# All K loads before all V loads in a decode-attention kernel, with one shared buffer pool and a split last V

## The chip, the cores and the metric

The kernel runs on one core of a Trainium2 chip. The metric is the device time of one execution in microseconds. Most executions of a kernel agree closely; a profiled execution also has a *span*, from its first to its last instruction, which in this case is 1.7 to 2.9 us shorter than the time of the same run. Times inside a run are counted from the start of its span; landings of loads are worked out from the semaphore marks in the trace, which the profile's own views do not list.

Short names: TensorE (PE) does matrix products, a *pair* is one weight load with its matmul; VectorE (DVE) and ScalarE (ACT) copy results and do the softmax; SyncE (SP) issues the loads; 16 DMA engines carry them out.

## The reference, cut to what matters

```python
B, D, Hq, Hkv, Sk, Dh = 32, 512, 32, 8, 2048, 128      # everything bfloat16
W = 512                                                # only the last 512 positions count
q = (x @ wq)                                           # 32 batches, one query each, 32 heads
k = k_cache[:, :, Sk - W:, :]; v = v_cache[:, :, Sk - W:, :]
p = softmax(q @ k.T * Dh ** -0.5)                      # 4 query heads share one K/V group
out = (p @ v) @ wo
```

Per batch 1 MB of K and 1 MB of V are read, besides 4 MB for wq and 4 MB for wo: 75.5 MB in all, each byte used once. Inside a group the 128 KB are contiguous; the kernel gives each of the 128 partitions four positions of a group, so a contiguous piece (a *row* of the load) is 1 KB.

## The kernel before

For every batch TensorE transposes K (32 pairs), VectorE and ScalarE copy the result (tile `kT_ps`) to `kT` (4 copies), and TensorE multiplies it with the queries (8 matmuls, "scores"). After every fourth batch (a *block*) the softmax runs on 128 rows at once, P is transposed (4 pairs), and PV is computed (32 pairs per batch). K and V have separate buffers, and their loads alternate:

```python
NK, NV = 4, 10                       # K buffers, V buffers, 1 MB each
# SyncE: k1, k2, k3, v0, k4, v1, ... then the last 5 K, then the last 8 V
for b in range(1, KSPLIT):           # KSPLIT = B - 5
    order.append(("k", b))
    if b >= VLAG: order.append(("v", b - VLAG))        # VLAG = 3
    if b == WO_AFTER: order.append(("wo", 0))          # WO_AFTER = 10
for b in range(KSPLIT, B): order.append(("k", b))
for b in range(KSPLIT - VLAG, B): order.append(("v", b))
# ... load_k(b) waits until K b-4 is transposed, load_v(b) until PV b-10 is done

# TensorE, program order
for s in range(0, 26):
    transposes(s + 2); scores(s)
    # s == 4*kb+4: ptrans(kb);  s == 4*kb+5: pv(kb), 4 batches at once
transposes(28); scores(26); oproj_A()                  # projection of batches 0 to 23
transposes(29); scores(27)
transposes(30); scores(28); ptrans(6)
transposes(31); scores(29); scores(30); scores(31)
pv(6); oprojT(6); ptrans(7); pv(7); oprojT(7)          # oprojT: 128 pairs for one block
out_transposes()
```

## Time and profile before

| | before |
|---|---|
| time, first four runs | 237.24 us median (237.09 to 238.6) |
| span of the profiled run | 234.7 us |
| TensorE matmul busy | 75% of the span |
| read from memory | 75.53 MB |

From the page: three rows of its slices (the span in 40 equal slices of 5.87 us: TensorE's granted clock in tenths, the busy share of the DMA engines in tenths, and GB/s), and the summary of the chain of work that ended last.

```profile
PEclk9975899989997558999799799979889999999755
DMA  6999999999999999999999999999999999999100
GB/s 214 413 393 348 350 349 348 351 348 348 351 353 348 349 348 351 349 349 349 349 350 348 351 348 350 348 350 348 349 350 348 350 349 349 348 338 339 64 6 1
...
DMA 56%; PE 36%; issue 3%; DVE 3%; SPq 0%; ACT 0%; DVEq 0%
```

The DMA engines have no pause from slice 2 to slice 37. With 8 KB rows (wq, slices 2 and 3) they move about 400 GB/s (418 to 430 between 8 and 14 us), with 1 KB rows 348 to 353 (338 and 339 in slices 36 and 37). Then come three slices with almost no load: a tail.

In the trace every load leaves 16 marks on its semaphore, and the kernel lets TensorE start on the data only when it has counted all 16. The marks of the last V load lie between 216.96 and 220.88 us (the prediction below has both 0.10 us later): the last mark is 3.9 us behind the first, and TensorE may start on this V only at 220.88. This spread, which the prediction calls skew, differs from load to load: 1.0 us for the load that landed at 25.7 us, 5.1 at most (landed at 206.2). The span ends at 234.7, 13.8 us later.

From the timeline of the kernel before, its end (columns: start us, duration us, engine, line, operation, output<-inputs, shapes, count; in brackets how long the engine idled before, and what released it):

```profile
210.71 5.13 PE L239 MATMUL sc_ps<-kT,L 128*128 128x512 bf16 x23
...
215.67 3.35 PE L268 MATMUL m_ps<-pT,vbuf 128*128 128x4 bf16 x128
...
219.41 3.56 PE L296 MATMUL m_ps<-oT_sb,wbuf 128*128 128x4 bf16 x128 [0.39 <-DVE oT_sb L450]
...
222.83 0.59 PE L253 MATMUL pT_ps<-ident,P 128*128 128x128 bf16 x4
223.45 0.60 ACT L381 ACTIVATE pT<-pT_ps 128x512 bf16<-128x512 bf16 x1 [5.89 <-PE pT_ps L253]
...
224.10 3.58 PE L268 MATMUL m_ps<-pT,vbuf 128*128 128x4 bf16 x128 [0.69 <-ACT pT L381]
...
228.07 3.58 PE L296 MATMUL m_ps<-oT_sb,wbuf 128*128 128x4 bf16 x128 [0.39 <-DVE oT_sb L450]
...
231.93 0.59 PE L309 MATMUL pT_ps<-ident,oT_sb 128*8 128x128 bf16 x4 [0.28 <-DVE oT_sb L458]
232.55 0.41 DVE L460 COPY out_sb<-pT_ps 8x512 bf16<-8x512 bf16 x1 [0.68 <-PE pT_ps L309]
232.99 0.31 SPq L169 DMA_DIRECT2D out_dram<-out_sb  x1
```

L239 is the score work of batches 29 to 31, L268 is PV of blocks 6 and 7, L296 the projection of a block, L253 the transposes of P. The scores end at 215.84. PV of block 7 starts at 224.10, three microseconds after its last V has landed. So the last byte is not what the end waited for: TensorE had its own queue of work, and it was late.

### The profile page before, as it was taken

How to read it: one execution, taken by the hardware profiler on the slowest of the kernel's cores; microseconds unless marked ns; L12 is line 12 of the kernel's file. 1: busy time of each engine (PE TensorE's matmuls, PEld its weight loads, DVE VectorE, ACT ScalarE, POOL GpSimd, SP SyncE). 2: the span in 40 equal slices, each digit the busy share in tenths (PEclk: the TensorE clock that was granted, in tenths of full speed). 3: DMA queues.
4: the chain of work that ended last, by engine and by line, in shares of the span. 5: the costliest groups of instructions: out<-in, count | busy, mean ns of one | idle time of the engine just before them, and what ended most of it. 6: DMA issues, size and time to landing. Idle time of an engine off the chain costs nothing.

```text
span 234.7 us, 6022 instructions
## 1 busy us (share of the span) xinstructions
PE 174.9 (75%) x2738; PEld 135.2 (58%) x2760; DVE 78.3 (33%) x147; ACT 46.3 (20%) x59; POOL 8.2 (4%) x9
## 2 busy tenths in 40 slices
PE   0606789689766019966996889669897699999985
PEld 0506767468544018744874567456865495675975
DVE  0303245532452003453334433453245330481101
ACT  2110331321132001132112221132033210141010
POOL 7600000000000000000000000000000000000000
PEclk9975899989997558999799799979889999999755
DMA  6999999999999999999999999999999999999100
GB/s 214 413 393 348 350 349 348 351 348 348 351 353 348 349 348 351 349 349 349 349 350 348 351 348 350 348 350 348 349 350 348 350 349 349 348 338 339 64 6 1
DMA packets 71308, 75.94 MB, mean 324 GB/s; under 512 B 1092, under 2 KB 70756, under 8 KB 70772
## 3 DMA queue, kind: packets, MB, share of 16 engines
q1 hardware_dynamic: 71252, 75.53, 99.9%
q8 instruction: 21, 0.34, 0.6%
q0 software_dynamic: 32, 0.03, 0.0%
q14 instruction: 3, 0.02, 0.0%
HBM read 75.53 MB, written 0.03 MB: 322 GB/s over the span
## 4 chain that ended last, share of the span: by engine, by line
DMA 56%; PE 36%; issue 3%; DVE 3%; SPq 0%; ACT 0%; DVEq 0%
DMA kbuf<-in_k_cache_dram 56%; PE sc_ps L239 10%; PE kT_ps L221 10%; PE m_ps L268 8%; PE m_ps L296 3%; PE sc_ps L282 3%; DVE kT L410 2%; PE sc_ps L198 1%; DVE oT_sb L450 0%; ACT pT L381 0%; PE pT_ps L309 0%; DVE out_sb L454 0%; SPq L141 0%; PE pT_ps L253 0%; SPq L122 0%
## 5 line engine op out<-in xcount | busy, mean ns | idle before, releaser
L221 PE MATMUL kT_ps<-ident,kbuf 128*128 128x128 bf16 x1024 | 73.7, 238 | 44.7 <-DMA kbuf<-in_k_cache_dram 41.9
L221 PEld LDWEIGHTS kT_ps<-ident,kbuf 128*128 128x128 bf16 x1024 | 67.8, 108 | 52.9 <-DMA kbuf<-in_k_cache_dram 48.4
L410 DVE COPY kT<-kT_ps 128x1024 bf16<-128x1024 bf16 x96 | 61.5, 686 | 81.5 <-issue 42.1
L239 PE MATMUL sc_ps<-kT,L 128*128 128x512 bf16 x234 | 59.4, 394 | 3.6 <-DVE kT L410 1.6
L355 ACT ACTIVATE kT<-kT_ps 128x1024 bf16<-128x1024 bf16 x32 | 32.7, 1023 | 137.5 <-PE kT_ps L221 119.5
L239 PEld LDWEIGHTS sc_ps<-kT,L 128*128 128x128 bf16 x256 | 25.2, 103 | 27.7 <-issue 5.8
L268 PEld LDWEIGHTS m_ps<-pT,vbuf 128*128 128x128 bf16 x1024 | 27.0, 97 | 2.6 <-ACT pT L381 1.0
L268 PE MATMUL m_ps<-pT,vbuf 128*128 128x4 bf16 x1024 | 27.0, 164 | 0.7 <-ACT pT L381 0.7
L450 DVE CAST oT_sb<-m_ps 128x128 bf16<-128x128 f32 x8 | 2.3, 292 | 36.4 <-PE m_ps L268 36.4
L432 DVE TENSOR_REDUCE mx<-sc_ps 128x1 f32<-128x512 f32 x8 | 5.5, 692 | 12.4 <-PE sc_ps L239 12.4
L367 ACT ACTIVATE E_sb<-sc_ps,nmx 128x512 f32<-128x512 f32 x8 | 5.5, 687 | 16.0 <-DVE nmx L434 16.0
L381 ACT ACTIVATE pT<-pT_ps 128x512 bf16<-128x512 bf16 x8 | 4.8, 597 | 15.3 <-PE pT_ps L253 15.3
L296 PE MATMUL m_ps<-oT_sb,wbuf 128*128 128x4 bf16 x256 | 7.1, 168 | 0.8 <-DVE oT_sb L450 0.8
L296 PEld LDWEIGHTS m_ps<-oT_sb,wbuf 128*128 128x128 bf16 x256 | 7.0, 103 | 0.9 <-DVE oT_sb L450 0.9
L282 PE MATMUL sc_ps<-wbuf,oT_sb 128*24 128x512 bf16 x32 | 7.1, 380 | 0.0
L190 PE MATMUL pT_ps<-ident,x_sb 32*128 32x32 bf16 x4 | 0.3, 182 | 7.6 <-DMA x_sb<-in_x_dram 7.6
L282 PEld LDWEIGHTS sc_ps<-wbuf,oT_sb 128*24 128x24 bf16 x32 | 3.7, 119 | 3.3 <-issue 0.4
L190 PEld LDWEIGHTS pT_ps<-ident,x_sb 32*128 32x128 bf16 x4 | 0.2, 102 | 7.6 <-issue 7.6
L443 DVE TENSOR_SCALAR P<-E_sb,rs 128x512 bf16<-128x512 f32 x8 | 3.9, 486 | 0.3
L424 DVE COPY L<-qT_sb 128x128 bf16<-128x128 bf16 x8 | 2.1, 262 | 4.5 <-ACT qT_sb L344 4.5
L439 DVE RECIPROCAL rs<-ssum 128x1 f32<-128x1 f32 x8 | 1.3, 164 | 6.8 <-ACT E_sb L367 6.8
L198 PEld LDWEIGHTS sc_ps<-xT_sb,wbuf 128*128 128x128 bf16 x128 | 3.5, 102 | 0.0
(22 smaller groups left out, 25.4 us busy)
## 6 DMA issues: line engine op xcount, KB each, us to landing
kbuf<-in_k_cache_dram SPq DMA_DIRECT2D x32, 1024.0 KB, 12.0
vbuf<-in_v_cache_dram SPq DMA_DIRECT2D x32, 1024.0 KB, 12.1
wbuf<-in_wq_dram SPq DMA_DIRECT2D x1, 4096.0 KB, 15.4
wbuf<-in_wo_dram SPq DMA_DIRECT2D x1, 4096.0 KB, 20.7
x_sb<-in_x_dram POOLq DMA_DIRECT2D x1, 32.0 KB, 6.2
out_dram<-out_sb SPq DMA_DIRECT2D x1, 24.0 KB
out_dram<-out_sb SPq DMA_DIRECT2D x1, 8.0 KB
```

The lines of the kernel that those rows point to most:

```text
L198: ins = pe.matmul(sc_ps[:, h * B:(h + 1) * B], wbuf[:, t * (H * DH) + h * DH: t * (H * DH) + (h + 1) * DH], xT_sb[:, t * B:(t + 1) * B], s ...
L221: ins = pe.transpose(dst, src, ident[:, :])
L239: ins = pe.matmul(sc_ps[:, half * 512:(half + 1) * 512], L[blk % 2][:, (bl * 8 + g) * 128:(bl * 8 + g + 1) * 128], kT_sb[b % NKT][:, g * W ...
L268: ins = pe.matmul(m_ps[:, reg * 128 + bl * 32 + 4 * g: reg * 128 + bl * 32 + 4 * g + 4], vbuf[vslot][:, g * W + j * 128: g * W + (j + 1) * ...
L282: ins = pe.matmul(sc_ps[0:NB_A, 512:1024], bass.AP(oT_sb, h, [[B * H, 128], [H, NB_A]]), wbuf[:, h * D:(h + 1) * D], start=(h == 0), stop= ...
L296: ins = pe.matmul(m_ps[:, c * 4 * NQ + 4 * q: c * 4 * NQ + 4 * q + 4], wbuf[:, h * D + c * 128: h * D + (c + 1) * 128], bass.AP(oT_sb, 4 * ...
L355: act.activation(kT_sb[b % NKT][:, c * 1024:(c + 1) * 1024], kT_ps[:, bank * 1024:(bank + 1) * 1024], ACTF.Copy,).then_inc(sem_act_kT, 1)
L367: act.activation(E_sb[:, :], sc_ps[:, half * 512:(half + 1) * 512], ACTF.Exp, bias=nmx[kb % 2][:, 0:1], scale=1.0, accum_out=ssum[kb % 2][ ...
L381: act.activation(pT_sb[kb % 2][:, :], pT_ps[:, 0:W], ACTF.Copy).then_inc(sem_act_pT, 1)
L410: dve.tensor_copy(kT_sb[b % NKT][:, c * 1024:(c + 1) * 1024], kT_ps[:, bank * 1024:(bank + 1) * 1024],).then_inc(sem_dve_kT, 1)
L432: dve.tensor_reduce(mx[kb % 2][:, 0:1], sc_ps[:, half * 512:(half + 1) * 512], AXX, ALU.max).then_inc(sem_dve_loc, 1)
L443: dve.tensor_scalar(P_sb[kb % 2][:, :], E_sb[:, :], rs[kb % 2][:, 0:1], None, ALU.mult).then_inc(sem_dve_P, 1)
```

## The change

Its intent: take all score and softmax work out of the end, so that after the last byte there is as little left as possible.

- All 32 K are loaded first, then wo, then all 32 V, from one pool of 14 buffers that K and V share.
- TensorE does all scores first. The transposed P of all 8 blocks is kept (8 buffers in place of 2), then PV follows for all batches. The last 8 batches get one output projection of 128 pairs in place of two, one for each block.
- The last four V are loaded by halves of the groups: first halves of all four, then second halves. This projection is done for the first 16 heads while the second halves arrive, and for the last 16 heads after that; VectorE adds the two parts.
- Max, exponential and normalisation of a block are placed one batch later.

```diff
-NK = 4
-NV = 10
+NKV = 14
...
-            # k and v alternate, the last 5 K before the last 8 V
+            for b in range(1, B):
+                load_k(b)
+            # wo here
+            for b in range(B - 4):
+                load_v(b)
+            for hf in range(2):
+                for q in range(4):
+                    b = B - 4 + q
+                    # groups 4*hf to 4*hf+3 of V b, own semaphore for each half
...
+            def wait_slot_free(i):              # i: 0..31 the K, 32..63 the V
+                j = i - NKV
+                if j < 0: return
+                if j < B: sp.wait_ge(sem_pe_kT, 4 * j + 4)        # K j transposed
+                else:     sp.wait_ge(sem_pe_pv, (j - B) + 1)      # PV j-32 done
...
             for s in range(0, B):
                 if s + LAGT < B: transposes(s + LAGT)      # LAGT = 2
                 scores(s)
-                # s == 4*kb+4: ptrans(kb);  s == 4*kb+5: pv(kb)
+                # s == 4*kb+5: ptrans(kb)
-            # late scores, oproj_A, pv(6), oprojT(6), ptrans(7), pv(7), oprojT(7)
+            ptrans(NBLK - 1)
+            for b in range(B - 4):
+                pv(b)
+                if b == 24: oprojT(0, 6)        # batches 0 to 23
+            for hf in range(2):
+                for b in range(B - 4, B):
+                    pv(b, range(4 * hf, 4 * hf + 4))
+                oproj_half(hf)                  # 16 heads, 8 batches: 64 pairs
             out_transposes()
...
-                    if b == 4 * kb + 5:         # VectorE: max of a block
+                    if b == 4 * kb + 3 + LAGT + 1:
```

More of the change, by code (lines that the diff above doesn't have):

```diff
@@ L15 @@
 NBLK = B // 4
-NK = 4
+NKV = 14
 NKT = 3
-NV = 10
 NKT_PS = 4
-VLAG = 3
-WO_AFTER = 10
-LAG1 = 1
-LAG2 = 2
-NB_A = 24
-NQ = (B - NB_A) // 4
+LAGT = 2
+LAGP = 2
 BF16 = mybir.dt.bfloat16
@@ L51, in bass_standalone__sliding_block_cached__sampling_kernel @@
         wbuf = sb("wbuf", [128, DT * H * DH], BF16)
-        kbuf = [sb(f"kbuf{i}", [128, G * W], BF16) for i in range(NK)]
+        kvbuf = [sb(f"kv{i}", [128, G * W], BF16) for i in range(NKV)]
         kT_sb = [sb(f"kT{i}", [128, G * W], BF16) for i in range(NKT)]
-        vbuf = [sb(f"vbuf{i}", [128, G * W], BF16) for i in range(NV)]
         L = [sb(f"L{i}", [128, 32 * 128], BF16) for i in range(2)]
@@ L61, in bass_standalone__sliding_block_cached__sampling_kernel @@
         P_sb = [sb(f"P{i}", [128, W], BF16) for i in range(2)]
-        pT_sb = [sb(f"pT{i}", [128, W], BF16) for i in range(2)]
+        pT_sb = [sb(f"pT{i}", [128, W], BF16) for i in range(NBLK)]
         oT_sb = sb("oT_sb", [128, B * H], BF16)
+        hA_sb = sb("hA_sb", [128, 32], FP32)
+        outT_sb = sb("outT_sb", [128, 4 * B], BF16)
         out_sb = sb("out_sb", [128, D], BF16)
-        out_sb2 = sb("out_sb2", [128, D], BF16)
-        oT2_sb = sb("oT2_sb", [128, 4 * (B - NB_A)], BF16)
         mx = [sb(f"mx{i}", [128, 8], FP32) for i in range(2)]
@@ L80, in bass_standalone__sliding_block_cached__sampling_kernel @@
         sem_out = sem("sem_out")
-        sem_k = [sem(f"sem_k{i}") for i in range(NK)]
-        sem_v = [sem(f"sem_v{i}") for i in range(NV)]
+        sem_kv = [sem(f"sem_kv{i}") for i in range(NKV)]
+        sem_vh = [sem(f"sem_vh{i}") for i in range(4)]
         sem_pool = sem("sem_pool")
@@ L87, in bass_standalone__sliding_block_cached__sampling_kernel @@
         sem_pe_pv = sem("sem_pe_pv")
+        sem_pe_op = sem("sem_pe_op")
         sem_pe_misc = sem("sem_pe_misc")
@@ L112, in evac_count, with k_slot, v_slot, slot_use_count @@
             return (n // 4) * 3 + (n % 4) + 1
+        def k_slot(b):
+            return b % NKV
+        def v_slot(b):
+            return (B + b) % NKV
+        def slot_use_count(i):
+            return i // NKV + 1
         @block.sync
         def _(sp):
+            def wait_slot_free(i):
+                j = i - NKV
+                if j < 0:
+                    return
+                if j < B:
+                    sp.wait_ge(sem_pe_kT, 4 * j + 4)
+                else:
+                    sp.wait_ge(sem_pe_pv, (j - B) + 1)
             def load_k(b):
-                slot = b % NK
-                if b >= NK:
-                    sp.wait_ge(sem_pe_kT, 4 * (b - NK) + 4)
+                i = b
+                wait_slot_free(i)
                 src = k_cache[b, :, SK - W:, :].rearrange("g (p r) d -> p g (r d)", p=128)
-                dst = kbuf[slot][:, :].rearrange("p (g x) -> p g x", g=G)
-                sp.dma_start(dst, src).then_inc(sem_k[slot], 16)
+                dst = kvbuf[i % NKV][:, :].rearrange("p (g x) -> p g x", g=G)
+                sp.dma_start(dst, src).then_inc(sem_kv[i % NKV], 16)
             def load_v(b):
-                slot = b % NV
-                if b >= NV:
-                    sp.wait_ge(sem_pe_pv, b - NV + 1)
+                i = B + b
+                wait_slot_free(i)
                 src = v_cache[b, :, SK - W:, :].rearrange("g (p r) d -> p g (r d)", p=128)
-                dst = vbuf[slot][:, :].rearrange("p (g x) -> p g x", g=G)
-                sp.dma_start(dst, src).then_inc(sem_v[slot], 16)
-            def load_wo():
-                sp.wait_ge(sem_pe_misc, 2)
-                sp.wait_ge(sem_act_misc, 2)
-                sp.dma_start(
-                    wbuf[:, :].rearrange("p (h n) -> p h n", h=H),
-                    wo.rearrange("(h p) n -> p h n", p=128),
-                ).then_inc(sem_wo, 16)
+                dst = kvbuf[i % NKV][:, :].rearrange("p (g x) -> p g x", g=G)
+                sp.dma_start(dst, src).then_inc(sem_kv[i % NKV], 16)
             load_k(0)
@@ L144, in _ @@
             ).then_inc(sem_wq, 16)
-            order = []
-            KSPLIT = B - 5
-            for b in range(1, KSPLIT):
-                order.append(("k", b))
-                if b >= VLAG:
-                    order.append(("v", b - VLAG))
-                if b == WO_AFTER:
-                    order.append(("wo", 0))
-            for b in range(KSPLIT, B):
-                order.append(("k", b))
-            for b in range(KSPLIT - VLAG, B):
-                order.append(("v", b))
-            assert len(order) == len(set(order)) == 2 * B
-            for kind, b in order:
-                if kind == "k":
-                    load_k(b)
-                elif kind == "v":
-                    load_v(b)
-                else:
-                    load_wo()
-            outv = out.rearrange("b o d -> (b o) d")
-            sp.wait_ge(sem_dve_out, 1)
-            sp.dma_start(outv[0:NB_A, :], out_sb[0:NB_A, :]).then_inc(sem_out, 16)
-            sp.wait_ge(sem_dve_out, 3)
-            sp.dma_start(outv[NB_A:B, :], out_sb2[0:B - NB_A, :]).then_inc(sem_out, 16)
-            sp.wait_ge(sem_out, 32)
+            for b in range(1, B):
+                load_k(b)
+            sp.wait_ge(sem_pe_misc, 2)
+            sp.wait_ge(sem_act_misc, 2)
+            sp.dma_start(
+                wbuf[:, :].rearrange("p (h n) -> p h n", h=H),
+                wo.rearrange("(h p) n -> p h n", p=128),
+            ).then_inc(sem_wo, 16)
+            for b in range(B - 4):
[3 more added lines that the diff above has]
+                    b = B - 4 + q
+                    i = B + b
+                    if hf == 0:
+                        wait_slot_free(i)
+                    src = v_cache[b, 4 * hf:4 * hf + 4, SK - W:, :].rearrange("g (p r) d -> p g (r d)", p=128)
+                    dst = kvbuf[i % NKV][:, 4 * hf * W:4 * (hf + 1) * W].rearrange("p (g x) -> p g x", g=4)
+                    sp.dma_start(dst, src).then_inc(sem_kv[i % NKV] if hf == 1 else sem_vh[q], 16)
+            sp.wait_ge(sem_dve_out, 2)
+            sp.dma_start(out.rearrange("b o d -> (b o) d"), out_sb[0:B, :]).then_inc(sem_out, 16)
+            sp.wait_ge(sem_out, 16)
         @block.gpsimd
@@ L207, in transposes @@
             def transposes(b):
-                slot = b % NK
-                pe.wait_ge(sem_k[slot], 16 * (b // NK + 1))
+                slot = k_slot(b)
+                pe.wait_ge(sem_kv[slot], 16 * slot_use_count(b))
                 for c in range(4):
@@ L218, in transposes @@
                         j = i % 4
-                        src = kbuf[slot][:, g * W + j * 128: g * W + (j + 1) * 128]
+                        src = kvbuf[slot][:, g * W + j * 128: g * W + (j + 1) * 128]
                         dst = kT_ps[:, bank * 1024 + i * 128: bank * 1024 + (i + 1) * 128]
@@ L232, in scores @@
                         pe.wait_ge(sem_act_exp, blk - 1)
-                    if b == NB_A + 4:
-                        pe.wait_ge(sem_dve_out, 1)
                 for g in range(G):
@@ L254, in ptrans, with pv @@
                 ins.then_inc(sem_pe_pT, 1)
-            def pv(kb, bls=(0, 1, 2, 3)):
+            def pv(b, gs=range(G)):
+                kb, bl = divmod(b, 4)
                 reg = kb % 4
-                if bls[0] == 0:
+                if bl == 0:
                     pe.wait_ge(sem_act_pT, kb + 1)
-                    if kb >= 4:
-                        pe.wait_ge(sem_dve_oT, kb - 3)
-                for bl in bls:
-                    b = 4 * kb + bl
-                    vslot = b % NV
-                    pe.wait_ge(sem_v[vslot], 16 * (b // NV + 1))
-                    for g in range(G):
-                        for j in range(KT):
-                            ins = pe.matmul(
-                                m_ps[:, reg * 128 + bl * 32 + 4 * g: reg * 128 + bl * 32 + 4 * g + 4],
-                                vbuf[vslot][:, g * W + j * 128: g * W + (j + 1) * 128],
-                                pT_sb[kb % 2][:, j * 128 + bl * 32 + 4 * g: j * 128 + bl * 32 + 4 * g + 4],
-                                start=(j == 0),
-                                stop=(j == KT - 1),
-                            )
-                    ins.then_inc(sem_pe_pv, 1)
@@ L277, in oproj_A @@
-            def oproj_A():
-                pe.wait_ge(sem_dve_oT, NB_A // 4)
-                pe.wait_ge(sem_wo, 16)
-                pe.wait_ge(sem_act_exp, NB_A // 4)
-                for h in range(H):
-                    ins = pe.matmul(
-                        sc_ps[0:NB_A, 512:1024],
-                        bass.AP(oT_sb, h, [[B * H, 128], [H, NB_A]]),
-                        wbuf[:, h * D:(h + 1) * D],
-                        start=(h == 0),
-                        stop=(h == H - 1),
-                    )
-                ins.then_inc(sem_pe_misc, 1)
@@ L291, in oprojT @@
-            def oprojT(kb):
-                pe.wait_ge(sem_dve_oT, kb + 1)
-                q = kb - (NBLK - NQ)
+                    if kb >= 1:
+                        pe.wait_ge(sem_dve_oT, kb)
+                vslot = v_slot(b)
+                if gs[-1] == 3:
+                    pe.wait_ge(sem_vh[bl], 16)
+                else:
+                    pe.wait_ge(sem_kv[vslot], 16 * slot_use_count(B + b))
+                for g in gs:
+                    for j in range(KT):
+                        ins = pe.matmul(
+                            m_ps[:, reg * 128 + bl * 32 + 4 * g: reg * 128 + bl * 32 + 4 * g + 4],
+                            kvbuf[vslot][:, g * W + j * 128: g * W + (j + 1) * 128],
+                            pT_sb[kb][:, j * 128 + bl * 32 + 4 * g: j * 128 + bl * 32 + 4 * g + 4],
+                            start=(j == 0),
+                            stop=(j == KT - 1),
+                        )
@@ L294, in oprojT @@
+                ins.then_inc(sem_pe_pv, 1)
+            def oprojT(k0, k1):
+                pe.wait_ge(sem_dve_oT, k1)
+                if k0 == 0:
+                    pe.wait_ge(sem_wo, 16)
+                    pe.wait_ge(sem_act_exp, NBLK)
+                n = 4 * (k1 - k0)
                 for c in range(4):
@@ L296, in oprojT @@
                         ins = pe.matmul(
-                            m_ps[:, c * 4 * NQ + 4 * q: c * 4 * NQ + 4 * q + 4],
+                            sc_ps[:, c * B + 4 * k0: c * B + 4 * k1],
                             wbuf[:, h * D + c * 128: h * D + (c + 1) * 128],
-                            bass.AP(oT_sb, 4 * kb * H + h, [[B * H, 128], [H, 4]]),
+                            bass.AP(oT_sb, 4 * k0 * H + h, [[B * H, 128], [H, n]]),
                             start=(h == 0),
@@ L302, in oprojT, with oproj_half @@
                         )
-                ins.then_inc(sem_pe_misc, 1)
+                ins.then_inc(sem_pe_op, 1)
+            def oproj_half(hf):
+                pe.wait_ge(sem_dve_oT, NBLK + hf)
+                for c in range(4):
+                    o = c * B + 24 if hf == 1 else 512 + 8 * c
+                    for h in range(16 * hf, 16 * hf + 16):
+                        ins = pe.matmul(
+                            sc_ps[:, o:o + 8],
+                            wbuf[:, h * D + c * 128: h * D + (c + 1) * 128],
+                            bass.AP(oT_sb, 24 * H + h, [[B * H, 128], [H, 8]]),
+                            start=(h % 16 == 0),
+                            stop=(h % 16 == 15),
+                        )
+                ins.then_inc(sem_pe_op, 1)
@@ L305, in out_transposes @@
             def out_transposes():
-                pe.wait_ge(sem_dve_out, 2)
-                nr = B - NB_A
+                pe.wait_ge(sem_dve_out, 1)
                 for c in range(4):
-                    ins = pe.transpose(pT_ps[0:nr, c * 128:(c + 1) * 128], oT2_sb[:, c * nr:(c + 1) * nr], ident[:, :])
+                    ins = pe.transpose(pT_ps[0:B, c * 128:(c + 1) * 128], outT_sb[:, c * B:(c + 1) * B], ident[:, :])
                 ins.then_inc(sem_pe_misc, 1)
             xT()
-            transposes(0)
@@ L314, in _ @@
-            transposes(1)
+            for b in range(LAGT):
+                transposes(b)
             qproj()
-            S_GEN = NB_A + 2
-            for s in range(0, S_GEN):
-                transposes(s + 2)
+            for s in range(0, B):
+                if s + LAGT < B:
+                    transposes(s + LAGT)
                 scores(s)
-                for kb in range(NB_A // 4):
-                    if s == 4 * kb + 3 + LAG1:
+                for kb in range(NBLK):
+                    if s == 4 * kb + 3 + LAGP:
@@ L322, in _ @@
                         ptrans(kb)
-                    if s == 4 * kb + 3 + LAG2:
-                        pv(kb)
-            transposes(28); scores(26); oproj_A()
-            transposes(29); scores(27)
-            transposes(30); scores(28); ptrans(6)
-            transposes(31); scores(29); scores(30); scores(31)
-            pv(6)
-            oprojT(6)
-            ptrans(7)
-            pv(7, (0,)); pv(7, (1,)); pv(7, (2,)); pv(7, (3,))
-            oprojT(7)
+            ptrans(NBLK - 1)
@@ L334, in _ @@
+            for b in range(B - 4):
+                pv(b)
+                if b == 24:
+                    oprojT(0, 6)
+            for hf in range(2):
+                for b in range(B - 4, B):
+                    pv(b, range(4 * hf, 4 * hf + 4))
+                oproj_half(hf)
             out_transposes()
@@ L377, in pt_evac @@
                 act.wait_ge(sem_pe_pT, kb + 1)
-                if kb >= 2:
-                    act.wait_ge(sem_pe_pv, 4 * (kb - 2) + 4)
-                    act.wait_ge(sem_act_pT, kb - 1)
-                act.activation(pT_sb[kb % 2][:, :], pT_ps[:, 0:W], ACTF.Copy).then_inc(sem_act_pT, 1)
+                act.activation(pT_sb[kb][:, :], pT_ps[:, 0:W], ACTF.Copy).then_inc(sem_act_pT, 1)
             xt_evac()
-            evac(0, 3)
-            evac(1, 3)
+            for b in range(LAGT):
+                evac(b, 3)
             qt_evac()
-            for b in range(2, B):
-                evac(b, 3)
+            for b in range(LAGT, B + 8):
+                if b < B:
+                    evac(b, 3)
                 for kb in range(NBLK):
-                    if b == 4 * kb + 5:
+                    if b == 4 * kb + 3 + LAGT + 1:
                         exp_block(kb)
-                    if b == 4 * kb + 5 + LAG1:
+                    if b == 4 * kb + 3 + LAGT + 1 + LAGP:
                         pt_evac(kb)
-            exp_block(7)
-            pt_evac(7)
         @block.vector
@@ L450, in ot_evac, with out_final @@
                 dve.tensor_copy(oT_sb[:, kb * 128:(kb + 1) * 128], m_ps[:, reg * 128:(reg + 1) * 128]).then_inc(sem_dve_oT, 1)
-            def out_evac_A():
-                dve.wait_ge(sem_pe_misc, 3)
-                dve.tensor_copy(out_sb[0:NB_A, :], sc_ps[0:NB_A, 512:1024]).then_inc(sem_dve_out, 1)
-            def out_last():
-                dve.wait_ge(sem_pe_misc, 3 + NQ)
-                dve.tensor_copy(oT2_sb[:, :], m_ps[:, 0:4 * (B - NB_A)]).then_inc(sem_dve_out, 1)
-                dve.wait_ge(sem_pe_misc, 4 + NQ)
-                dve.tensor_copy(out_sb2[0:B - NB_A, :], pT_ps[0:B - NB_A, 0:512]).then_inc(sem_dve_out, 1)
+            def out_final():
+                dve.wait_ge(sem_dve_loc, loc[0])
+                dve.wait_ge(sem_pe_op, 3)
+                dve.tensor_tensor(
+                    bass.AP(outT_sb, 24, [[4 * B, 128], [B, 4], [1, 8]]),
+                    bass.AP(sc_ps, 24, [[1024, 128], [B, 4], [1, 8]]),
+                    bass.AP(hA_sb, 0, [[32, 128], [8, 4], [1, 8]]),
+                    ALU.add,
+                ).then_inc(sem_dve_out, 1)
+                dve.wait_ge(sem_pe_misc, 3)
+                dve.tensor_copy(out_sb[0:B, :], pT_ps[0:B, 0:512]).then_inc(sem_dve_out, 1)
             def E(b):
@@ L464, in E @@
                     evac(b, c)
-            E(0)
-            E(1)
+            for b in range(LAGT):
+                E(b)
             lcopy(0)
-            for b in range(2, B):
+            for b in range(LAGT, B + 8):
                 for kb in range(NBLK):
-                    if b == 4 * kb + 6:
+                    if b == 4 * kb + 3 + LAGT + 2:
                         norm_block(kb)
-                    if b == 4 * kb + 5 + LAG2 + 1 and kb < NB_A // 4:
-                        ot_evac(kb)
-                if b == NB_A + 5:
-                    out_evac_A()
-                E(b)
+                if b < B:
+                    E(b)
                 for kb in range(NBLK):
-                    if b == 4 * kb + 5:
+                    if b == 4 * kb + 3 + LAGT + 1:
                         max_block(kb)
                 for blk in range(1, NBLK):
-                    if b == max(2, 4 * blk - 2):
+                    if b == max(LAGT, 4 * blk - 2):
                         lcopy(blk)
-            max_block(7)
-            norm_block(7)
-            ot_evac(6)
-            ot_evac(7)
-            out_last()
+            for kb in range(NBLK - 1):
+                ot_evac(kb)
+            for hf in range(2):
+                dve.wait_ge(sem_pe_pv, 4 * NBLK - 4 + 4 * (hf + 1))
+                o7 = (NBLK - 1) * 128
+                dst = bass.AP(oT_sb, o7 + 16 * hf, [[B * H, 128], [H, 4], [1, 16]])
+                src = bass.AP(m_ps, 3 * 128 + 16 * hf, [[512, 128], [32, 4], [1, 16]])
+                dve.wait_ge(sem_dve_oT, NBLK - 1 + hf)
+                dve.tensor_copy(dst, src).then_inc(sem_dve_oT, 1)
+                if hf == 0:
+                    dve.wait_ge(sem_pe_op, 2)
+                    loc[0] += 2
+                    dve.tensor_copy(
+                        bass.AP(outT_sb, 0, [[4 * B, 128], [B, 4], [1, 24]]),
+                        bass.AP(sc_ps, 0, [[1024, 128], [B, 4], [1, 24]]),
+                    ).then_inc(sem_dve_loc, 1)
+                    dve.tensor_copy(hA_sb[:, :], sc_ps[:, 512:544]).then_inc(sem_dve_loc, 1)
+            out_final()
 _INS = ['x', 'k_cache', 'v_cache', 'wq', 'wo']
```

## The prediction

> **What bounds it now.** The page's slices show the DMA engines busy at 99% from slice 2 to 37 at a steady 348 to 351 GB/s; only the 8 KB rows of wq went faster (about 420). The chain of waits is 56% DMA into kbuf and 36% PE. So the body is a stream of 75.5 MB at the rate of 1 KB packets, and what is left is the tail. In the trace the sixteen completion marks of the last V load (batch 31) lie from 217.06 to 220.98 us. [...] The span ends at 234.7: 13.7 us after the last byte. The timeline of those 13.7: TensorE still has the block-6 output projection (3.56), then four transposes of P (0.59), their copy (0.60), PV of the whole block 7 (3.58), copy (0.29), block-7 projection (3.58), copy, transposes, copy (0.20+0.60+0.41), store (1.7). It was late because the last K loads come late and the score work of batches 28 to 31 runs until 215.8.
>
> **What the change does.** Same bytes, same packet size. All K first, then wo, all V; one pool of 14 buffers. All score and softmax work leaves the tail. The last four V are split by heads, so that after the last landing only 16 PV pairs and a half projection (64 pairs) remain.
>
> **K stage.** It turns from DMA-bound to PE-bound: one batch costs 1.96 (transposes) + 1.67 (scores) with overlap, 3.5 us start to start in the undisturbed stretch 32 to 39 us, against 3.0 us per MB of DMA. Max and norm sit one batch later, so that the DVE no longer holds the transposes back. Starting scores at 30.5: 29 x 3.5 + 5 + 3 for the P transposes gives the end of scores at about 140, the first PV at about 144. DMA runs ahead of PE into the V's. V14 is the first load that waits for a PV; in an unbroken stream it is issued at about 152. So there are 8 us of slack, plus about 9 us that are queued: no hole in the DMA unless a batch takes over about 4.1 us.
>
> **V stage.** PV is 0.85 us per batch against 3.0 of DMA: DMA-bound; PE is caught up well before the end.
>
> **Tail, estimated.** Last landing again about 221 (same bytes, same engines, same skew). Then PV 0.6, copy 0.35, 64 pairs at 28 ns and the latency 2.0, add 0.25, transposes 0.65, copy 0.46, store to end 1.75: 6.1 us in place of 13.7. The clock falls to half in the tail (0.50 from 220 us on)[...]; but 128 four-column pairs took 3.58 us there against 3.35 at full clock, so it costs little.
>
> Span 227.1; the timed runs are 2.5 above the span: **229.6 us**, 3.2% less. Range 227.2 to 232.2. Chances: faster 0.90, same 0.08, slower 0.02.
>
> **What would show it.** Right: GB/s still about 349 in slices 2 to 36; kT transposes end near 135 and are hardly released by K loads; last V landing at 220 to 222; chain: DMA, then about 6 us; scores of a batch in about 3.5 us. Wrong if: DMA dips near slices 25 to 28 (V slots not free, PE too slow[...]); the last landing moves by more than 1 us (other engine skew, or the split loads slower); the tail over 7 us.

What is marked as cut in the recorded texts, here and below, was shown by no trace or run of this case. No term of the tail's sum is among it: 0.6 + 0.35 + 2.0 + 0.25 + 0.65 + 0.46 + 1.75 is the 6.1 us.

## The result, and the profile after

| | before | after |
|---|---|---|
| time, median | 238.53 us (237.09 to 240.52, 16 runs) | 228.81 us (228.5 to 229.36, 11 runs) |
| span, profiled run | 234.7 us | 226.9 us |
| last V landing (16th mark) | 220.88 us | 220.74 us |
| last landing to end of span | 13.8 us | 6.2 us |
| end of all scores | 215.84 us | 138.87 us |

The ratio is 0.9586 (95% interval 0.9556 to 0.9616): 4.1% faster. Ratios here are the mean time of one kernel's fast runs over that of the other's fast runs in the same rounds, so they are not quite the ratio of the medians quoted.

The same rows of the page for the changed kernel (slices of 5.67 us):

```profile
PEclk9975899999999999999999999755555555555555
DMA  6999999999999999999999999999999999999950
GB/s 210 417 398 348 348 349 348 349 348 349 349 349 348 348 348 349 348 349 348 349 348 350 350 347 348 348 350 350 350 351 349 348 348 348 339 348 338 351 168 9
...
PE 47%; DMA 33%; SPq 10%; issue 6%; DVE 3%; DVEq 0%
```

The rate of the stream is the same within a few GB/s, and so is its end. Only the empty slices behind it have shrunk from three to about one.

The end of the changed kernel in the timeline:

```profile
220.24 1.14 PE L267 MATMUL m_ps<-pT,kv 128*128 128x4 bf16 x34 [1.49 <-issue]
...
221.41 0.22 DVE L486 CAST oT_sb<-m_ps 128x64 bf16<-128x64 f32 x1 [3.06 <-PE m_ps L267]
...
221.69 1.88 PE L298 MATMUL sc_ps<-oT_sb,wbuf 128*128 128x8 bf16 x64 [0.32 <-DVE oT_sb L486]
223.67 0.19 DVE L450 TENSOR_TENSOR outT_sb<-sc_ps,hA_sb 128x32 bf16<-128x32 f32 x1 [2.04 <-PE sc_ps L298]
...
223.92 0.61 PE L310 MATMUL pT_ps<-ident,outT_sb 128*32 128x128 bf16 x4 [0.35 <-DVE outT_sb L450]
224.56 0.41 DVE L457 COPY out_sb<-pT_ps 32x512 bf16<-32x512 bf16 x1 [0.70 <-PE pT_ps L310]
225.00 0.37 SPq L168 DMA_DIRECT2D out_dram<-out_sb  x1
```

L267 is PV, L298 the projection of 16 heads. After the landing at 220.74 the last PV pairs end at 221.38, the copy takes 0.22, the 64 pairs 1.88, and so on to the store at 225.00. No softmax, no score and no full projection is left here.

The K stage, in windows (columns: stretch, its length, busy us and count of PE, weight loads, DVE, ACT, POOL, then granted clock, DMA share, GB/s):

```profile
30.00:60.00 30.00, 29.74 (x332) 21.62 (x335) 16.98 (x30) 10.47 (x12) 0.00 (x0) 1.00 1.10 348
60.00:90.00 30.00, 29.79 (x350) 22.33 (x353) 19.24 (x40) 11.50 (x16) 0.00 (x0) 1.00 1.10 349
90.00:120.00 30.00, 29.79 (x341) 21.96 (x343) 19.55 (x38) 11.45 (x15) 0.00 (x0) 1.00 1.10 349
...
145.00:160.00 15.00, 6.88 (x224) 6.46 (x224) 0.58 (x2) 0.00 (x0) 0.00 (x0) 0.50 1.10 350
```

TensorE is busy 29.8 of 30 us, at full clock: this stage has become TensorE-bound, at about 3.57 us per batch (from the scores of batch 2 at 37.32 us to those of batch 28 at 130.00) against 3.0 us of loading, and the stream runs ahead of it. In the V stage TensorE is busy 6.9 of 15 us at a granted clock of 0.50, and the stream is what it waits for (34.1 us of PV's waits in this run end with a V load).

### The profile page after: what moved, and what is told of

Same layout as the page of the kernel before. It is cut to its first block, busy times and chain, and to the rows that moved or that the text cites. A ratio compares the mean times of both kernels' runs of the same rounds, so it can differ in the third digit from the quotient of the medians.

```text
span 226.9 us, 5965 instructions
## 1 busy us (share of the span) xinstructions
PE 161.9 (71%) x2712; PEld 129.5 (57%) x2728; DVE 76.4 (34%) x149; ACT 45.7 (20%) x59; POOL 8.2 (4%) x9
## 4 chain that ended last, share of the span: by engine, by line
PE 47%; DMA 33%; SPq 10%; issue 6%; DVE 3%; DVEq 0%
DMA kv<-in_v_cache_dram 25%; PE sc_ps L236 22%; PE kT_ps L220 20%; DMA kv<-in_k_cache_dram 8%; SPq L141 8%; DVE kT L405 2%; SPq L166 2%; PE m_ps L267 2%; PE sc_ps L298 2%; PE sc_ps L197 1%; PE pT_ps L310 0%; SPq L144 0%; DVE oT_sb L486 0%; SPq L134 0%; DVE out_sb L457 0%
## 5 line engine op out<-in xcount | busy, mean ns | idle before, releaser
L220 PE MATMUL kT_ps<-ident,kv 128*128 128x128 bf16 x1024 | 65.7, 225 | 10.1 <-DMA kv<-in_k_cache_dram 8.3
L220 PEld LDWEIGHTS kT_ps<-ident,kv 128*128 128x128 bf16 x1024 | 62.5, 101 | 15.9 <-DMA kv<-in_k_cache_dram 8.5
L267 PE MATMUL m_ps<-pT,kv 128*128 128x4 bf16 x1024 | 31.6, 166 | 39.9 <-DMA kv<-in_v_cache_dram 34.1
L236 PE MATMUL sc_ps<-kT,L 128*128 128x512 bf16 x240 | 56.9, 379 | 0.8
L267 PEld LDWEIGHTS m_ps<-pT,kv 128*128 128x128 bf16 x1024 | 29.6, 103 | 42.5 <-DMA kv<-in_v_cache_dram 26.5
L236 PEld LDWEIGHTS sc_ps<-kT,L 128*128 128x128 bf16 x256 | 23.7, 98 | 22.9
L427 DVE TENSOR_REDUCE mx<-sc_ps 128x1 f32<-128x512 f32 x8 | 5.5, 682 | 4.2 <-PE sc_ps L236 4.2
L284 PE MATMUL sc_ps<-oT_sb,wbuf 128*128 128x24 bf16 x128 | 5.9, 218 | 0.6 <-issue 0.6
L284 PEld LDWEIGHTS sc_ps<-oT_sb,wbuf 128*128 128x128 bf16 x128 | 5.6, 122 | 0.0
L250 PEld LDWEIGHTS pT_ps<-ident,P 128*128 128x128 bf16 x32 | 2.4, 98 | 4.6 <-DVE P L438 3.0
L250 PE MATMUL pT_ps<-ident,P 128*128 128x128 bf16 x32 | 3.1, 219 | 2.5 <-DVE P L438 2.5
L298 PE MATMUL sc_ps<-oT_sb,wbuf 128*128 128x8 bf16 x128 | 3.8, 175 | 0.6 <-DVE oT_sb L486 0.6
L298 PEld LDWEIGHTS sc_ps<-oT_sb,wbuf 128*128 128x128 bf16 x128 | 3.6, 103 | 0.8 <-DVE oT_sb L486 0.8
```

The costliest lines, as they stand in the source:

```text
L220: ins = pe.transpose(dst, src, ident[:, :])
L236: ins = pe.matmul(sc_ps[:, half * 512:(half + 1) * 512], L[blk % 2][:, (bl * 8 + g) * 128:(bl * 8 + g + 1) * 128], kT_sb[b % NKT][:, g * W ...
L250: ins = pe.transpose(pT_ps[:, j * 128:(j + 1) * 128], P_sb[kb % 2][:, j * 128:(j + 1) * 128], ident[:, :])
L267: ins = pe.matmul(m_ps[:, reg * 128 + bl * 32 + 4 * g: reg * 128 + bl * 32 + 4 * g + 4], kvbuf[vslot][:, g * W + j * 128: g * W + (j + 1) ...
L284: ins = pe.matmul(sc_ps[:, c * B + 4 * k0: c * B + 4 * k1], wbuf[:, h * D + c * 128: h * D + (c + 1) * 128], bass.AP(oT_sb, 4 * k0 * H + h ...
L298: ins = pe.matmul(sc_ps[:, o:o + 8], wbuf[:, h * D + c * 128: h * D + (c + 1) * 128], bass.AP(oT_sb, 24 * H + h, [[B * H, 128], [H, 8]]), ...
```

## The experiments

### The split of the last V

`a_whole_v` leaves the last four V loads whole:

```diff
-            for b in range(B - 4): load_v(b)
-            for hf in range(2): ...              # halves
+            for b in range(B): load_v(b)
...
-            for hf in range(2):
-                for b in range(B - 4, B): pv(b, range(4 * hf, 4 * hf + 4))
-                oproj_half(hf)
+            for b in range(B - 4, B): pv(b)
+            oprojT(6, 8)                         # 128 pairs
```

> The changed kernel with the last four V loads left whole, so that after the last landing 32 PV pairs and the projection of 8 batches (128 pairs) remain in place of 16 and 64. Tail theory (the gain is work taken off the 13.7 us after the last byte; the load stream is untouched): last landing still 220 to 222, tail 6.1 + 0.5 (16 more pairs) + 1.9 (64 more pairs) = 8.4 to 8.6 us, time about 231.2 (0.5 us of it uncertain). Rival, the stream itself got better by the order and the shared pool and the split is decoration: within 0.5 us of 228.8.

Measured: 231.11 us, ratio to the kernel before 0.971 (0.9665 to 0.9755). The last landing was at 220.70 and the span 229.0: a tail of 8.3 us. The end of its timeline:

```profile
220.75 1.01 PE L258 MATMUL m_ps<-pT,kv 128*128 128x4 bf16 x32 [1.68 <-DMA kv<-in_v_cache_dram]
221.80 0.29 DVE L435 CAST oT_sb<-m_ps 128x128 bf16<-128x128 f32 x1 [11.27 <-PE m_ps L258]
...
222.15 3.58 PE L275 MATMUL sc_ps<-oT_sb,wbuf 128*128 128x8 bf16 x128 [0.39 <-DVE oT_sb L435]
...
227.10 0.36 SPq L159 DMA_DIRECT2D out_dram<-out_sb  x1
```

The split is therefore worth 2.3 us (231.11 against 228.81), mostly the 64 pairs that moved before the last landing (3.58 against 1.88 us). The rest of the gain, 238.4 to 231.1, comes from the new order and what was changed with it: the shared pool and the place of the softmax (tested below) and the single projection of the last 8 batches. That last one has no run of its own: in the kernel before, 2.1 us of the projection of block 6 lay after the last landing (until 222.97), and how much of the gain is its merging and how much the order is not shown.

### The size of the pool

`b_pool8` and `b_pool6` change one number: `NKV = 14` to 8 and to 6.

> The changed kernel with 8 shared buffers in place of 14. Tail theory with the slack reckoning: the first load that waits for a PV is now V8; the first PV runs at 142.5 and V8 would land at about 149 in an unbroken stream, [...]no hole: 228.5 to 230. Rival (the deep shared pool is what gained): several us slower, toward the time of the kernel before.

> 6 shared buffers. V6 waits for the first PV at 142.5, natural landing about 143[...]: one hole of about 4 us in GB/s near 140 to 147, then the stream at full rate again if 6 buffers keep about 4 MB in flight: time 232 to 234, last landing about 225. If the model of the slack is wrong: no change, or a loss over 8 us.

Measured: 229.96 us with 8 buffers (229.05 to 230.66), 235.97 us with 6. With 8, the cost is about 1 us: nearly all of the gain is kept at little over half of the memory. So a deep pool is not what gained (the kernel before had 4 and 10 buffers, 14 too). The time is as expected, but "no hole" is not: in the profiled run, one of the two longer ones (230.66), the rate falls to 342, 337, 300 and 284 GB/s in slices 16 to 19 (86 to 109 us), and the last V lands at 222.42. With 6 the loss is 7.2 us, more than the 3 to 5 expected, and it lies elsewhere (6 buffers, the kernel before: ratio 0.9915). The GB/s row of the page with 6 buffers (slices of 5.84 us):

```profile
GB/s 219 418 390 348 349 347 348 348 348 347 348 326 303 298 312 287 284 319 275 322 350 348 349 348 349 349 349 348 348 348 349 348 347 349 347 350 346 347 183 6
```

The hole is not near 140 to 147 us (slices 25 and 26, 349 GB/s both), where the first PV frees a V buffer. It lies between slice 12 and slice 20, 64 to 117 us: there TensorE is the slower partner, and with 6 buffers the K loads are held to its pace (they waited 72.8 us in all for transposes, 37.6 with 14). The last K landed at 117.0 us; with 14 buffers it was 111.8. The last V landed at 227.58, 6.8 us later than with 14, and the span is longer by the same 6.8 us: that is the whole loss. The expectations for both pools had reckoned with about 4.5 us from issue to landing (with 6 buffers 142.5 to 147). That was an estimate which no trace shows, and with 8 buffers "no hole" rested on it; the shortest 1 MB load of the run with 6 took 5.3. They had also looked only at the stage border, not at the K stage itself, where the reader is slower than the loader for 100 us. The model of the slack was too simple; that slack exists with 14 buffers stands.

### The place of the softmax

`d_softmax_early` puts max, exponential, normalisation and the transposes of P back by one batch, as the kernel before had them:

```diff
-LAGP = 2
+LAGP = 1
...
-  if b == 4 * kb + 3 + LAGT + 1:   # max, exponential
+  if b == 4 * kb + 3 + LAGT:
-  if b == 4 * kb + 3 + LAGT + 2:   # normalisation
+  if b == 4 * kb + 3 + LAGT + 1:
```

> The changed kernel with max, exponential, normalisation and P transposes one batch earlier, as the kernel before had them, so that VectorE waits for the scores inside the K stage again (about 1.3 us per block, 8 blocks). Tail theory: the end of the scores moves from 138.9 to about 147, still before the stream needs a V buffer back (first waiting load issued at about 152), so last landing about 221 and time 228.5 to 229.5. Rival (a smoother TensorE schedule in the K stage is part of the gain): 4 to 9 us slower.

Measured: 228.86 us, no difference. But the reason is not the slack that the expectation named: the K stage did not get longer at all. The end of the scores in the changed kernel, and then in this experiment (L236 scores, L427 the max of the last block, L250 transposes of P, L267 the first PV):

```profile
135.47 3.40 PE L236 MATMUL sc_ps<-kT,L 128*128 128x512 bf16 x15
138.90 0.69 DVE L427 TENSOR_REDUCE mx<-sc_ps 128x1 f32<-128x512 f32 x1 [4.20 <-PE sc_ps L236]
...
141.37 0.40 PE L250 MATMUL pT_ps<-ident,P 128*128 128x128 bf16 x4 [2.50 <-DVE P L438]
...
141.60 3.39 PE L267 MATMUL m_ps<-pT,kv 128*128 128x4 bf16 x128
```

```profile
138.87 0.69 DVE L427 TENSOR_REDUCE mx<-sc_ps 128x1 f32<-128x512 f32 x1 [4.58 <-PE sc_ps L236]
...
141.33 0.47 PE L250 MATMUL pT_ps<-ident,P 128*128 128x128 bf16 x4 [2.50 <-DVE P L438]
...
141.60 3.60 PE L267 MATMUL m_ps<-pT,kv 128*128 128x4 bf16 x128
```

The last max starts at 138.90 in the one and 138.87 in the other, and from 30 to 138 us TensorE is busy for 107.16 of the 108 us in both. The 1.3 us per block that VectorE was said to cost do not exist in this kernel.

### Why the kernel before varies

The kernel before took 236.4 to 240.5 us over all runs but one (below), with spans from 234.6 to 238.1. The changed kernel's spans in its runs lie between 226.7 and 227.4. Three unchanged copies of the kernel before were run to see where the difference sits.

> An unchanged copy of the kernel before. Its runs so far spread from 237.1 to 240.5 with a span of 234.7 in the profiled one, the changed kernel's only from 228.5 to 229.4. If the spread is in the kernel (late landings, other tail), the spans of these runs vary with the times by the same 3 us; if it is outside the kernel, the spans stay near 234.7 while the times vary.

> The kernel before, unchanged, for another profile: its spans over the runs are 234.6 to 236.7, and the profile shown so far (234.7) is at the short end, the changed kernel's are 226.7 to 227.4. Theory: the last V landing is again near 221 and the longer span is TensorE work (transposes and scores of the last batches) at half clock, so that the score work ends later than 215.8 by the difference, up to 2 us. Rival: the last landing itself is later by up to 2 us and the score work ends as before.

> As f_before_2, a third profile, because the span of one run cannot be chosen: whichever has a span near 236.4 decides between later landings and slower score work.

`f_before_again` gave 320.52, 238.3, 239.13 and 237.22 us. The spans of the three fast ones are 236.5, 236.4 and 234.9: they follow the times broadly, so most of the spread is in the kernel. Its profile fell on the run of 320 us: the 128x512 score matmuls took 722 ns (median) in place of 379, through the whole run. Its views show a granted clock of 1.00, but the trace holds no clock record for this run at all, and 1.00 is only what the views show where there is none. It is one run of its kind, and is used for no comparison.

`f_before_2` and `f_before_3` (240.34 and 239.85 us) had spans of 238.1 and 237.8. Each is a single run, so its state on record is "unknown", and what follows is a reading of two executions. In `f_before_2` the last V landed at 221.37 (0.5 us later than in the first profile), in `f_before_3` at 220.72 (0.2 us earlier). But the scores ended at 219.24 and 218.98, in place of 215.84. The two windows that differ, first of the kernel before in its first profile, then of `f_before_2` (granted clock third from the end):

```profile
186.00:197.00 11.00, 10.89 (x187) 7.82 (x187) 2.85 (x6) 2.05 (x2) 0.00 (x0) 1.00 1.10 349
```

```profile
186.00:197.00 11.00, 10.90 (x179) 8.66 (x180) 3.31 (x6) 1.78 (x2) 0.00 (x0) 0.71 1.10 349
```

And the pieces in the timeline in which the time was lost, first profile and then `f_before_2`:

```profile
185.87 1.89 PE L239 MATMUL sc_ps<-kT,L 128*128 128x512 bf16 x7
...
190.80 1.95 PE L221 MATMUL kT_ps<-ident,kbuf 128*128 128x128 bf16 x32
```

```profile
186.63 3.07 PE L239 MATMUL sc_ps<-kT,L 128*128 128x512 bf16 x7
...
192.76 3.39 PE L221 MATMUL kT_ps<-ident,kbuf 128*128 128x128 bf16 x32
...
214.11 5.13 PE L239 MATMUL sc_ps<-kT,L 128*128 128x512 bf16 x23
...
219.08 3.35 PE L268 MATMUL m_ps<-pT,vbuf 128*128 128x4 bf16 x128
```

The score matmuls of one batch (seven of the eight are recorded) took 3.07 us in place of 1.89 and 32 transposes 3.39 in place of 1.95, because the granted clock was lower for some microseconds (0.71 on average between 186 and 197 us, in place of 1.00). With the transposes before them (2.49 us in place of 1.96) these are 3.1 of the 3.4 us (for the size of the effect: in the kernel before, 32 transposes took 3.59 us at a granted clock of 0.50, from 19.75 us, and 1.96 at 1.00, from 201.44); the rest is the K load before them, which landed 0.3 us later. In `f_before_2` the chain that ended last is TensorE almost without a break from 184 us on: it starts when K 27 has landed (184.3 us) and runs through the rest of the scores, 7 us of projection for batches 0 to 23, PV and two more projections. So 54 us, nearly all of it TensorE work, had to follow the landing of a K, and every microsecond that the clock costs in there is a microsecond of the time.

Why the clock fell there is not shown. The wait for K 27 was 2.1 us long, and as long in the first profile, where the clock stayed at 1.00. What differs is this: the lengths of the clock record's pieces are multiples of 3.41 us (3.41 to 47.78 in the first profile), and in `f_before_2` the wait (182.22 to 184.34) lay inside one step (182.18 to 185.59), with a granted clock of 0.50 in the next; in the first profile (181.96 to 184.07) a border at 182.37, counted on in such steps from the start of that piece at 172.13, cut it. The 0.50 came back after 192.41, and the step before that (189.00 to 192.41) held almost nothing but PV pairs, with TensorE busy for 3.36 of its 3.41 us. `f_before_3` has the same two drops. Whether the place of the borders decides is not shown: no run moves them. In the changed kernel no such chain of score work ends the run.

### A longer row

The stream now bounds all but about 6 us. Its rate was 349 GB/s for 1 KB rows, and higher for wq (418 to 430 with its 8 KB rows). `e_k2k` reads K in rows of 2 KB: two groups share the 128 partitions, each with 64 partitions of eight positions.

```diff
-                src = k_cache[b, :, SK - W:, :].rearrange("g (p r) d -> p g (r d)", p=128)
-                dst = kvbuf[i % NKV][:, :].rearrange("p (g x) -> p g x", g=G)
-                sp.dma_start(dst, src).then_inc(sem_kv[i % NKV], 16)
+                for h in range(2):
+                    src = k_cache[b, h::2, SK - W:, :].rearrange("g (p r) d -> p g (r d)", p=64)
+                    dst = kvbuf[i % NKV][h::2, :].rearrange("p (g x) -> p g x", g=4)
+                    sp.dma_start(dst, src).then_inc(sem_kv[i % NKV], 16)
...                        # scores: the 512 columns of a group lie 2 apart
-                        kT_sb[b % NKT][:, g * W:(g + 1) * W],
+                        bass.AP(kT_sb[b % NKT], (g // 2) * 1024 + g % 2, [[G * W, 128], [128, 8], [2, 64]]),
...                        # P is written in the order in which V lies
-                dve.tensor_scalar(P_sb[kb % 2][:, :], E_sb[:, :], ...)
+                dve.tensor_scalar(
+                    bass.AP(P_sb[kb % 2], 0, [[W, 128], [1, 2], [128, 4], [2, 64]]),
+                    bass.AP(E_sb, 0, [[W, 128], [256, 2], [64, 4], [1, 64]]), ...)
```

`e_kv2k` does the same with V. There a V tile holds positions of two groups, so P is transposed with every column doubled, and two ScalarE copies with a mask as their scale set the other group's partitions to zero; one PV pair then serves 8 columns of two groups:

```diff
-NKV = 14
+NKV = 13
...
-                for j in range(KT):              # transposes of P
+                for j in range(2 * KT):
...
+                for h in range(2):               # mask[q, h] = 1 where q % 2 == h
+                    ins = act.activation(
+                        bass.AP(pT_sb[kb], 4 * h, [[2 * W, 128], [8, 128], [1, 4]]),
+                        bass.AP(pT_ps, 4 * h, [[1024, 128], [8, 128], [1, 4]]),
+                        ACTF.Copy, scale=mask[:, h:h + 1])
...
+                for gp in range(gs[0] // 2, (gs[-1] + 1) // 2):
+                    for r in range(2 * KT):      # one pair: two groups, 8 columns
```

> The changed kernel with K read in rows of 2 KB: 64 partitions per group, two groups share the 128 partitions (two loads per batch), the score columns put in order again when P is written. Correct result. If the stream is what the rest of the time hangs on and its rate depends on the row length: the trace has 47 ns per 1 KB row and engine (349 GB/s) and about 312 ns per 8 KB row (420 GB/s), a line through both gives 85 ns for 2 KB, 385 GB/s, K in 87 us in place of 96: last landing about 212, time about 220. If 349 GB/s is the memory's own limit and wq was fast for another reason: 228.5 to 229.5. If half-partition loads or the strided columns cost: slower.

> K and V both in rows of 2 KB; for V the transposed P is kept per pair of groups with zeros for the other group (8 P transposes and two masked copies per block), so that the count of PV pairs stays 32 per batch; 13 shared buffers in place of 14[...]. Correct result. With 385 GB/s on 67 MB: 18 us off the stream, last landing about 203 and time about 211, if the K stage (end of the scores about 140, first PV 143) lets V13 go in time: its issue would fall at about 135 to 140 in an unbroken stream with 9 us queued, so a small hole (0 to 4 us) is possible: 210 to 215. If the row length does not matter: 228.5 to 230.

Both results are correct. Measured: 220.06 us (ratio to the kernel before 0.9247) and 212.58 us (0.8942). The GB/s rows, `e_k2k` first (slices of 5.46 us), then `e_kv2k` (5.26 us):

```profile
GB/s 161 431 411 388 386 387 387 387 387 387 387 385 388 386 388 386 387 388 362 349 349 349 348 348 348 347 348 348 349 348 348 349 347 347 339 351 338 350 127 6
```

```profile
GB/s 168 427 413 389 388 386 385 387 388 387 388 387 385 387 386 387 387 387 385 352 349 375 389 381 390 383 387 362 311 385 385 385 385 385 386 385 386 385 88 6
```

With 2 KB rows the stream runs at 385 to 388 GB/s, in place of 348 to 350, exactly as long as such rows are read: until slice 18 in the first, and nearly throughout in the second (381 to 390). There the 349 around slice 21 is wo with its 1 KB rows. The 362 and 311 in slices 28 and 29 (142 to 152 us) are a hole: V loads wait for buffers until the first PV runs (145.57 us). The loads were also cut in two, to 512 KB each, but that alone does not do it: the last eight V loads of the changed kernel had 512 KB and 1 KB rows and ran at 338 to 351 (its slices 37 and 38).

In `e_k2k` the last V landed at 212.35 us, 8.4 earlier than in the changed kernel, and the tail stayed at 6.2: the faster stream arrives in the time in full. In `e_kv2k` the last V landed at 202.51, 18.2 us earlier, but the span is only 16.5 us shorter, because the tail grew to 7.9. Its timeline shows TensorE behind the stream (L303 is the half projection, L272 PV):

```profile
200.01 1.85 PE L303 MATMUL sc_ps<-oT_sb,wbuf 128*128 128x8 bf16 x63 [0.32 <-DVE oT_sb L502]
...
202.91 0.19 PE L303 MATMUL sc_ps<-oT_sb,wbuf 128*128 128x8 bf16 x1 [1.06 <-issue]
...
203.04 1.85 PE L272 MATMUL m_ps<-pT,kv 128*128 128x8 bf16 x64
```

The first half projection ends after the last landing, so all 64 pairs of the second PV halves still follow it. TensorE stood still before it, for 2.35 us until 197.25 and 1.06 us until 202.91, in waits that the views call "issue". Both end about 1.4 us after a 16 KB transfer of the DMA queue named "instruction" (until 195.87 and 201.54), as do two such waits of the changed kernel (until 213.78 and 220.24, transfers until 212.37 and 218.83); what TensorE waited for there is not shown. `e_kv2k` beats both kernels all the same.

## Why the prediction was right, point by point

- **The stream stays the same.** Right: 349 GB/s again, last landing 220.74 against a predicted "about 221".
- **The tail.** Right in sum and term by term: 6.1 us predicted and 6.2 us measured. PV after the landing 0.64 (0.6 predicted), the 64 pairs 1.88 (2.0 with latency), the time from the store to the end 1.9 (1.75).
- **The K stage is TensorE-bound without a hole.** Right with 14 buffers: scores ended at 138.87 (about 140 predicted), the first PV ran at 141.6 (144). The reckoning that gave "8 us of slack" is not confirmed as a method: with 6 buffers it put the hole at the wrong place and at about half its size.
- **"Max and norm sit one batch later, so that the DVE no longer holds the transposes back."** Wrong as a reason: with the old place the scores end at the same microsecond. It moved no time either way.
- **The size.** The time was predicted at 229.6 and is 228.81, inside the range. The saving was predicted at 7.6 us (3.2%); between the medians it is 9.7 us (4.1%). The spans of the two first profiles differ by 7.8 us, so the mechanism was sized well. The missing term is in the time *before*: the profiled run (237.35 us) was one of the shorter ones, 1.2 us under the median. In the two longer runs that have a profile TensorE falls 3.1 and 3.4 us behind, nearly all of it at a lower clock (0.71 and 0.73 on average between 186 and 197 us), on a chain of 50 us that ends the kernel, and the change takes that chain away; that the same makes the 1.2 us of the median is not shown. About 0.7 us more are in the step from span to time (1.9 us after, 2.65 before in the profiled runs), for which I have no cause.

The sentence of the prediction that the tail was late "because the last K loads come late" is right but too weak. K 31 landed at 195.9 and its scores ended at 215.8: the landing of K 27 at 184.0 started an unbroken chain of TensorE work, with a 7 us projection in the middle of it.

## What to carry to other kernels

When a stream of loads bounds the body, ask what must still be done after its last byte, and order the loads so that the data with the longest chain behind it come first; if the chain is much shorter, splitting the last loads takes a further part of it away. A faster compute stage should be worth nothing while it has slack (argued only: the run meant to test it left the stage as it was), and a deep pool little once it covers that slack; but look along the whole stage for it, not only at its end. Once only the stream is left, its rate pays nearly in full (8.4 of 8.4 us, then 16.5 of 18.2), as long as the work behind the last load keeps up: here longer rows gave a larger gain than the whole reordering (16.2 us against 9.7 between the medians).
